# A fused transformer block on one core: one of three small matrix-vector products leaves TensorE for VectorE

## The chip, the cores and the metric

The kernel runs on one core of one Trainium2 chip. The metric is device time in microseconds (us), one number for each execution. Executions of one kernel differ by a few tenths of a microsecond, so I quote medians.

## The reference

A DiT block: two layernorms, each modulated by a shift and a scale that come from a condition vector `c`, attention with two heads, and an MLP. Sizes are B=2, N=256 tokens, D=1152, F=4608.

```python
mod = (_silu(c) @ w_mod).reshape(B, 6, 1, D)
shift_a, scale_a, gate_a, shift_m, scale_m, gate_m = [mod[:, i] for i in range(6)]
h = _layernorm(x) * (1 + scale_a) + shift_a
q, k, v = split(h @ wqkv)                      # H = 2 heads, Dh = 576   (cut)
a = softmax(q k^T * Dh ** -0.5) v @ wo         # (cut)
x = x + gate_a * a
h2 = _layernorm(x) * (1 + scale_m) + shift_m
m = _gelu(h2 @ w_fc1) @ w_fc2
return x + gate_m * m
```

The change is about `mod`: six products of a 2 x 1152 matrix (two batch entries) with a 1152 x 1152 matrix. They need few multiplications, but each needs 2.65 MB of weights to pass through some engine.

## The kernel before

A small scheduler inside the kernel decides, at build time and by a cost model, the order of the instructions on VectorE, ScalarE and GpSimd. The order on TensorE and of the loads is that of the program text. `S.order_after(u, v)` adds a constraint by hand.

Three of the six products, gate_a, shift_m and scale_m, are made together on TensorE in `rows()`. The stationary operand is the two columns of silu(c). The weights stream past it. The 3456 output columns are dealt to four column tiles of the array (`tile_position`, j) and two PSUM banks (r), 448 at a time:

```python
RW = 448
def rows():
    for kt in range(KT):                               # KT = 9 slices of 128 input rows
        for r in range(2):
            for j in range(4):
                c0 = 2 * RW * j + RW * r
                n = min(RW, 3 * D - c0)
                bank = (3, 4)[r]
                mm(psum[32 * j:32 * j + 2, bank * 512:bank * 512 + n], ST[:, kt:18:9], WMODR[:, kt, c0:c0 + n],
                   kt == 0, kt == KT - 1, tile_position=(0, 32 * j))
    ...                                                # evict to ROWS; store gate_a, load it broadcast

def rows_T():                                          # shift_m, scale_m as columns: 18 tiny matmuls
    for i in range(2 * KT):
        j, o = (KT + i) // 7, (KT + i) % 7
        mm(ps32(5, i * 2, 2), ROWS[0:98, o * 128:(o + 1) * 128], IDENT[0:98, 32 * j:32 * j + 2], ...)
    ...                                                # SHM, and SC1M = 1 + scale_m
```

gate_m is already made on VectorE during the MLP, with one multiply-add over a 128 x 1152 slice for each of 9 slices and 2 batch entries:

```python
e.scalar_tensor_tensor(out=acc, in0=w, scalar=s, in1=acc, op0=ALU.mult, op1=ALU.add)   # acc f32, w bf16
```

Then `transpose` and `tensor_reduce` add up within groups of 32 partitions, and one small fp32 matmul adds the groups.

The order on TensorE is: K products; Q products; half products of attention (the 64-row rest of each head); scores and V products, mixed with the transposes of the softmax results; `rows`; the remaining V products and `rows_T`; attention times V; output projection Wo, mixed with the transposes of the second layernorm's tiles; the MLP.

## Time and profile before

| | before |
|---|---|
| time, median of 3 | 246.57 us (246.51 to 246.89) |
| span in the profile, granted clock | 244.6 us, 0.999 |
| busy: TensorE, VectorE, ScalarE | 98%, 40%, 26% |

The first lines of the page of the kernel before are busy time by engine (`PE` is TensorE, `PEld` its weight loads, `DVE` VectorE) and the chain of work that ended last:

```profile
span 244.6 us, 4029 instructions
## 1 busy us (share of the span) xinstructions
PE 239.7 (98%) x1751; PEld 147.4 (60%) x1761; DVE 97.9 (40%) x199; ACT 63.0 (26%) x126; POOL 21.3 (9%) x37
...
PE 95%; DVE 3%; POOL 1%; issue 1%; ACT 0%; DVEq 0%; POOLq 0%
```

TensorE is the bottleneck. Idle time on the other engines is free here, and a saving counts only if it is TensorE time. (In all views, `issue` is time in which an engine waited for nothing that the profile shows.)

The timeline of the kernel before, weight loads only, gives the start of each stage. The columns are start, duration, engine and line, operation, shapes, and in brackets the idle time before and what ended it. `64*128` are the half products, `128*2` the rows, `128*64` the first attention-times-V products; line L690 is a transpose, here the first tile of the second layernorm:

```profile
47.01 0.33 PEld L687 LDWEIGHTS psum<-arena 64*128 64x128 bf16 x8 [0.42 <-issue]
...
66.17 3.12 PEld L687 LDWEIGHTS psum<-arena 128*2 128x2 bf16 x72 [0.32 <-issue]
...
69.67 7.55 PEld L687 LDWEIGHTS psum<-arena 128*128 128x128 bf16 x63 [0.38 <-issue]
...
77.55 0.36 PEld L687 LDWEIGHTS psum<-arena 128*64 128x64 bf16 x8 [0.32 <-issue]
...
94.61 0.65 PEld L690 LDWEIGHTS psum<-arena 128*128 128x128 bf16 x9
```

The rows occupy TensorE from 66.17 to 69.67 us: 3.50 us for 72 matmuls. One after another, they would need about 13 us (an estimate: in this trace 512-wide matmuls start 0.216 us apart). So the tiles run side by side. That is what the Trainium skill, "TensorEngine Tiling (Array Packing)", section Key Properties, says: different tiles can execute weight loads and matmuls in parallel.

The timeline of VectorE shows the room there is. An eviction is the copy of a finished result out of PSUM. Before the Q evictions VectorE idles for 10.57 us:

```profile
45.18 2.63 DVE L684 CAST arena<-psum 128x512 bf16<-128x512 f32 x4 [10.57 <-PE psum L687]
```

The groups of instructions give the prices of the method used for gate_m (`|` busy us, mean ns `|` idle before):

```profile
L1044 DVE SCALAR_TENSOR_TENSOR arena<-arena 128x1152 f32<-128x1152 bf16 x16 | 22.7, 1416 | 0.5
L1048 DVE STREAM_TRANSPOSE arena<-arena 128x1152 f32<-128x1152 f32 x2 | 2.8, 1375 | 0.0
L1050 DVE TENSOR_REDUCE arena<-arena 128x72 f32<-128x2304 f32 x1 | 2.6, 2553 | 0.0
L1041 DVE TENSOR_SCALAR arena<-arena 128x1152 f32<-128x1152 bf16 x2 | 1.6, 812 | 0.0
```

### The profile page before, as it was taken

How to read it: one execution, taken by the hardware profiler on the slowest of the kernel's cores; microseconds unless marked ns; L12 is line 12 of the kernel's file. 1: busy time of each engine (PE TensorE's matmuls, PEld its weight loads, DVE VectorE, ACT ScalarE, POOL GpSimd, SP SyncE). 2: the span in 40 equal slices, each digit the busy share in tenths (PEclk: the TensorE clock that was granted, in tenths of full speed). 3: DMA queues.
4: the chain of work that ended last, by engine and by line, in shares of the span. 5: the costliest groups of instructions: out<-in, count | busy, mean ns of one | idle time of the engine just before them, and what ended most of it. 6: DMA issues, size and time to landing. Idle time of an engine off the chain costs nothing.

```text
span 244.6 us, 4029 instructions
## 1 busy us (share of the span) xinstructions
PE 239.7 (98%) x1751; PEld 147.4 (60%) x1761; DVE 97.9 (40%) x199; ACT 63.0 (26%) x126; POOL 21.3 (9%) x37
## 2 busy tenths in 40 slices
PE   7999999999999999999999999999999999999995
PEld 2698754556656756898544444444556656656575
DVE  3814360455313679879999600000022222111112
ACT  5730340244311306983322333222000000000000
POOL 1500000000021176500000000020000000000000
PEclk9999999999999999999999999999999999999999
DMA  6999999999992999989943589003000000000100
GB/s 242 332 381 392 391 390 406 419 419 405 385 323 66 339 377 392 392 295 398 350 133 97 181 285 343 0 3 96 0 16 19 16 16 20 16 16 16 32 19 19
DMA packets 28844, 51.59 MB, mean 211 GB/s; under 512 B 1559, under 2 KB 15643, under 8 KB 28827
## 3 DMA queue, kind: packets, MB, share of 16 engines
q1 hardware_dynamic: 28384, 50.14, 56.9%
q0 software_dynamic: 416, 1.19, 1.9%
q8 instruction: 14, 0.23, 0.4%
q14 instruction: 3, 0.02, 0.0%
q10 hardware_dynamic: 27, 0.00, 0.0%
HBM read 50.14 MB, written 1.19 MB: 210 GB/s over the span
## 4 chain that ended last, share of the span: by engine, by line
PE 95%; DVE 3%; POOL 1%; issue 1%; ACT 0%; DVEq 0%; POOLq 0%
PE psum L687 93%; PE psum L690 2%; DVE arena L734 1%; DVE arena L755 1%; POOL arena L738 0%; POOL arena L746 0%; DVE arena L735 0%; POOL arena L710 0%; DVE arena L800 0%; DVE arena L737 0%; DVE arena L1233 0%; DVE arena L1234 0%; POOL arena L709 0%; ACT arena L723 0%; DVE arena L724 0%
## 5 line engine op out<-in xcount | busy, mean ns | idle before, releaser
L687 PE MATMUL psum<-arena 128*128 128x384 bf16 (+11 forms) x1662 | 236.0, 309 | 2.0 <-POOL arena L710 1.4
L687 PEld LDWEIGHTS psum<-arena 128*128 128x128 bf16 (+2 forms) x1672 | 142.2, 97 | 91.8 <-issue 4.3
L1233 DVE TENSOR_TENSOR arena<-psum,arena 128x384 f32<-128x384 f32 (+3 forms) x14 | 7.0, 500 | 68.0 <-PE psum L687 68.0
L1143 ACT ACTIVATE arena<-psum 128x512 bf16<-128x512 f32 (+1 forms) x44 | 22.4, 519 | 42.7 <-PE psum L687 42.7
L684 DVE CAST arena<-psum 128x512 bf16<-128x512 f32 (+4 forms) x22 | 13.8, 633 | 31.8 <-PE psum L687 31.7
L682 ACT ACTIVATE arena<-psum 128x512 bf16<-128x512 f32 (+6 forms) x27 | 15.2, 578 | 38.0 <-PE psum L687 35.5
L1044 DVE SCALAR_TENSOR_TENSOR arena<-arena 128x1152 f32<-128x1152 bf16 x16 | 22.7, 1416 | 0.5
L1111 POOL TENSOR_TENSOR arena<-arena 128x384 f32<-128x384 f32 x12 | 10.9, 910 | 12.6 <-DVE arena L1110 10.4
L668 POOL DMA_DIRECT2D dit_scratch<-arena x3 | 1.8, 617 | 116.6 <-ACT arena L682 59.8
L734 DVE BATCH_NORM_STATS2 arena<-arena 128x6 f32<-128x384 f32 (+1 forms) x18 | 9.6, 549 | 0.0
L1056 DVE CAST arena<-psum 72x32 bf16<-72x32 f32 x1 | 0.2, 188 | 21.2 <-PE psum L687 21.2
L1110 DVE TENSOR_TENSOR arena<-psum,arena 128x384 f32<-128x384 f32 x12 | 6.7, 555 | 3.8 <-PE psum L687 3.8
L1116 ACT ACTIVATE arena<-arena 128x1152 bf16<-128x1152 f32 x4 | 5.3, 1344 | 9.8 <-DVE arena L1115 9.8
L690 PE MATMUL psum<-arena 128*128 128x128 bf16 (+1 forms) x89 | 7.3, 219 | 0.2
L690 PEld LDWEIGHTS psum<-arena 128*128 128x128 bf16 (+1 forms) x89 | 5.7, 98 | 2.6 <-DVE arena L755 0.9
L1234 DVE TENSOR_TENSOR arena<-arena 128x384 bf16<-128x384 f32 (+3 forms) x14 | 7.0, 500 | 0.5
L1133 ACT ACTIVATE arena<-psum,arena 128x128 bf16<-128x128 bf16 x16 | 6.1, 454 | 2.8 <-PE psum L690 2.2
L1130 DVE TENSOR_SCALAR arena<-psum,arena 128x128 bf16<-128x128 bf16 x20 | 5.5, 336 | 1.9 <-PE psum L690 1.9
L974 ACT ACTIVATE arena<-psum,arena 128x256 bf16<-128x256 f32 x8 | 3.7, 469 | 7.3 <-DVE arena L971 4.6
L970 DVE TENSOR_REDUCE arena<-psum 128x2 f32<-128x512 f32 x4 | 2.8, 692 | 2.6 <-PE psum L687 2.6
L738 POOL TENSOR_TENSOR arena<-arena 128x1 f32<-128x1 f32 x6 | 3.5, 576 | 1.1 <-DVE arena L737 1.1
L927 ACT ACTIVATE arena<-arena 128x256 bf16<-128x256 bf16 x6 | 2.5, 495 | 4.0 <-DVE arena L921 4.0
(45 smaller groups left out, 42.5 us busy)
## 6 DMA issues: line engine op xcount, KB each, us to landing
arena<-in_w_mod_dram SPq DMA_DIRECT2D x4, 2592.0 KB, 20.9
arena<-in_w_fc_dram SPq DMA_DIRECT2D x9, 1152.0 KB, 8.1
arena<-in_w_fc_dram SPq DMA_DIRECT2D x4, 2592.0 KB, 17.2
arena<-in_wqkv_dram SPq DMA_DIRECT2D x18, 288.0 KB, 11.0
arena<-in_w_mod_dram SPq DMA_DIRECT2D x3, 864.0 KB, 14.0
arena<-in_wqkv_dram SPq DMA_DIRECT2D x1, 2592.0 KB, 12.7
arena<-in_wo_dram SPq DMA_DIRECT2D x1, 2592.0 KB, 32.8
arena<-in_w_mod_dram SPq DMA_DIRECT2D x3, 480.0 KB, 10.2
```

Of the source, the lines that this page charges most:

```text
L682: act(c_act(n), lambda e: e.activation(out=dst, in_=src, func=ACTF.Copy), [src], [dst], name)
L684: dve(c_dve_psum16(n) if psum16 else c_dve_psum32(n), lambda e: e.tensor_copy(dst, src), [src], [dst], name)
L687: S.instr(lambda e: e.matmul(o, lhsT=l, rhs=r, start=st, stop=sp, **kw), reads=[l, r], writes=[o])
L690: S.instr(lambda e: e.transpose(o, i_, idn), reads=[i_, idn], writes=[o])
L734: dve(550, lambda e, s=s, o=o: e.bn_stats(out=o, in_=s), [s], [o], "bn_%s_%d" % (tag, ci))
L1044: dve(1270, lambda e, w=w, s=s, acc=acc: e.scalar_tensor_tensor(out=acc, in0=w, scalar=s, in1=acc, op0=ALU.mult, op1=ALU.add), [w, s, acc] ...
L1110: dve(550, lambda e, o=o, ga=ga, x1c=x1c: e.tensor_tensor(out=x1c, in0=o, in1=ga, op=ALU.mult), [o, ga], [x1c], "wo_t1_%d_%d" % (t, ci))
L1111: S.op("pool", 930, lambda e, xs=xs, x1c=x1c: e.tensor_tensor(out=x1c, in0=x1c, in1=xs, op=ALU.add), reads=[x1c, xs], writes=[x1c], name=" ...
L1133: act(440, lambda e, o=o, dst=dst, s1=s1, s2=s2: e.activation(out=dst, in_=o, func=ACTF.Identity, scale=s1, bias=s2), [o, s1, s2], [dst], ...
L1143: act(c_act(ntok), lambda e: e.activation(out=dst, in_=o, func=ACTF.Gelu_apprx_tanh), [o], [dst], "gelu_%d_%d" % (f, tok0))
L1233: dve(c_dve_psum32(w), lambda e, o=o, gm=gm, t1=t1: e.tensor_tensor(out=t1, in0=o, in1=gm, op=ALU.mult), [o, gm], [t1], "fc2_t1_%d_%d" % ( ...
L1234: dve(c_dve_32(w), lambda e, t1=t1, x1c=x1c, ost=ost: e.tensor_tensor(out=ost, in0=t1, in1=x1c, op=ALU.add), [t1, x1c], [ost], "fc2_out_%d ...
```

## The change

The intent is to take scale_m off TensorE. VectorE makes it with the gate_m method, in the stages where it had room: during Q, attention and V. TensorE's rows are left with gate_a and shift_m, 2304 columns, which split into eight pieces of 288. Order constraints place the multiply-adds between VectorE's other work. Two of VectorE's Q evictions and all of its V evictions go to ScalarE. The scale_m slices are loaded between the slices of WQ.

```diff
-        WMODR = wmat(O_R, 3 * D)
+        WMODR = wmat(O_R, 2 * D)
+        WSM = wmat(O_R + 3 * W1, D)
 ...
+        for o in (0, 640):
+            S.op("pool", 100, lambda e, o=o: e.memset(ROWS[:, o:o + 64], 0.0), ...)   # pads of ROWS
 ...
             dma(WQ[:, kt, :], wqkv_v[:, kt, 0:D], P * D * 2, "ld_wq%d" % kt, run=2304)
+            dma(WSM[:, kt, :], wmod_v[:, kt, 4 * D:5 * D], P * D * 2, "ld_sm%d" % kt, run=2304)
 ...
-        RW = 448
+        RW = 288
 ...
-            S.unit("pe", 2 * KT * 27.0, "rowsT")            # 18 matmuls
+            S.unit("pe", (KT + 1) * 27.0, "rowsT")          # 10 matmuls
 ...
+        def row_sums(W, acc2, t2, out, tag):                # the gate_m method, now for both
+            ...
+        def scale_m_columns():
+            p = ps32(0, 0, 72)
+            mm(p, QR, SMS, True, True)                      # fp32, adds the 4 groups of 32 partitions
+            ...                                             # 4 small VectorE ops write SC1M
 ...
+        for u in S.units:
+            if u.eng == "dve" and u.name.startswith("hx_"):
+                S.order_after(by["sm_0_0"], u)
+        for kt in range(KT):
+            S.order_after(by["sm_1_%d" % kt], by["sm_0_%d" % kt])
+        for j in (0, 2, 4):
+            S.order_after(by["qk_ev%d" % j], by["sm_1_2"])
+            S.order_after(by["sm_0_3"], by["qk_ev%d" % j])
+        S.order_after(by["smax_3"], by["sm_1_4"])
+        S.order_after(by["sm_0_5"], by["spn_3"])
+        ...                                                 # the half sums after the OT evictions
```

More of the change, by code (lines that the diff above doesn't have):

```diff
@@ L598, in build_kernel @@
         WV = wmat(O_C, D)
-        WMODR = wmat(O_R, 3 * D)
+        WMODR = wmat(O_R, 2 * D)
+        WSM = wmat(O_R + 3 * W1, D)
+        SMA = sb(O_R + 2 * W1, 9216, F32)
+        SMT = sb(O_R + 3 * W1 - 9216, 9216, F32)
         WGM = wmat(O_R + 3 * W1, D)
@@ L618, in build_kernel @@
         XN2 = [sb(O_R + 3 * W1 - (i + 1) * 2304, 2304) for i in range(4)]
-        ROWS = sb(O_R + 3 * W1 - 5 * 2304, 1792)
+        ROWS = sb(O_R + 2 * W1 + 9216, 2 * 704)
         GMA = sb(O_X, 9216, F32)
@@ L650, in build_kernel @@
         QS = sb(misc(128), 128, F32)
+        QR = sb(misc(512), 512, F32)
+        SMS = sb(misc(288), 288, F32)
         GMO = sb(misc(64), 64)
@@ L714, in build_kernel @@
         S.op("pool", 100, lambda e: e.memset(NHALF, -0.5), writes=[NHALF], name="nhalf")
+        for o in (0, 640):
+            S.op("pool", 100, lambda e, o=o: e.memset(ROWS[:, o:o + 64], 0.0), writes=[ROWS[:, o:o + 64]], name="rowpad%d" % o)
         dve(270, lambda e: e.memset(Q4B, 0.0), [], [Q4B], "zq4b")
@@ L726, in build_kernel @@
         dve(200, lambda e: e.tensor_reduce(out=QS, in_=i3, axis=AX.X, op=ALU.add), [IDENT], [QS], "qs")
+        q4 = QS.unsqueeze(1).broadcast_to([P, 4, 32])
+        dve(200, lambda e: e.tensor_copy(QR.rearrange("p (a i) -> p a i", a=4), q4), [QS], [QR], "qr")
         dve(170, lambda e: e.scalar_tensor_tensor(out=ST, in0=TH, scalar=1.0, in1=HC, op0=ALU.add, op1=ALU.mult), [TH, HC], [ST], "c_silu")
@@ L892, in qk_evac @@
         def qk_evac(j, bank):
-            copy_on("act" if ev_rr[0] % 2 == 0 else "dve", QK[:, j, :], ps32(bank), 512, False, "qk_ev%d" % j)
+            copy_on("act" if ev_rr[0] % 2 == 0 or j in (6, 8) else "dve", QK[:, j, :], ps32(bank), 512, False, "qk_ev%d" % j)
             ev_rr[0] += 1
@@ L918, in build_kernel @@
         for k0 in range(0, KT, 3):
-            dma(WMODR[:, k0:k0 + 3, :], wmod_v[:, k0:k0 + 3, 2 * D:5 * D], 3 * P * 3 * D * 2, "ld_modr%d" % k0)
+            dma(WMODR[:, k0:k0 + 3, :], wmod_v[:, k0:k0 + 3, 2 * D:4 * D], 3 * P * 2 * D * 2, "ld_modr%d" % k0)
         MT1 = ps32(2, 0, 18)
@@ L998, in v_proj @@
                 mm(o, HX[:, kt, t * 128:(t + 1) * 128], WV[:, kt, ci * CH:(ci + 1) * CH], kt == 0, kt == KT - 1)
-            copy_on("act" if v_rr[0] % 2 else "dve", V[:, t, ci * CH:(ci + 1) * CH], o, CH, False, "v_ev%d_%d" % (t, ci))
-        RW = 448
+            copy_on("act", V[:, t, ci * CH:(ci + 1) * CH], o, CH, False, "v_ev%d_%d" % (t, ci))
+        RW = 288
+        ROWP = 64
         def rows():
@@ L1009, in rows @@
                         c0 = 2 * RW * j + RW * r
-                        n = min(RW, 3 * D - c0)
                         bank = (3, 4)[r]
-                        mm(psum[32 * j:32 * j + 2, bank * 512:bank * 512 + n], ST[:, kt:18:9], WMODR[:, kt, c0:c0 + n],
+                        mm(psum[32 * j:32 * j + 2, bank * 512:bank * 512 + RW], ST[:, kt:18:9], WMODR[:, kt, c0:c0 + RW],
                            kt == 0, kt == KT - 1, tile_position=(0, 32 * j))
             for r, eng in ((0, "act"), (1, "dve")):
-                copy_on(eng, ROWS[0:98, r * RW:(r + 1) * RW], ps32(3 + r, 0, RW)[0:98, :], RW, False, "rows_ev%d" % r)
-            dma(scratch[0, :, 0:2 * RW], ROWS[0:2, :], 2 * 2 * RW * 2, "st_ga0", eng="pool")
-            dma(scratch[0, :, 2 * RW:D], ROWS[32:34, 0:D - 2 * RW], 2 * (D - 2 * RW) * 2, "st_ga1", eng="pool")
+                copy_on(eng, ROWS[0:98, ROWP + r * RW:ROWP + (r + 1) * RW], ps32(3 + r, 0, RW)[0:98, :], RW, False, "rows_ev%d" % r)
+            for j in range(2):
+                dma(scratch[0, :, 2 * RW * j:2 * RW * (j + 1)], ROWS[32 * j:32 * j + 2, ROWP:ROWP + 2 * RW], 2 * 2 * RW * 2, "st_ga%d" % j, eng="pool")
             gate_load(0, GA)
@@ L1024, in rows_T @@
         def rows_T():
-            S.unit("pe", 2 * KT * 27.0, "rowsT")
-            for i in range(2 * KT):
-                j, o = (KT + i) // 7, (KT + i) % 7
-                mm(ps32(5, i * 2, 2), ROWS[0:98, o * 128:(o + 1) * 128], IDENT[0:98, 32 * j:32 * j + 2], i == 0, i == 2 * KT - 1,
-                   skip_group_check=True)
-            a, b_ = ps32(5, 0, 18), ps32(5, 18, 18)
-            dve(170, lambda e: e.tensor_copy(SHM, a), [a], [SHM], "shm")
-            dve(170, lambda e: e.tensor_scalar(out=SC1M, in0=b_, scalar1=1.0, scalar2=None, op0=ALU.add), [b_], [SC1M], "sc1m")
+            S.unit("pe", (KT + 1) * 27.0, "rowsT")
@@ new lines, in rows_T @@
+            for i in range(KT):
+                for j in (2, 3):
+                    c0 = ROWP + 128 * i - 2 * RW * (j - 2)
+                    if -ROWP < c0 < ROWP + 2 * RW:
+                        mm(ps32(5, i * 2, 2), ROWS[0:98, c0:c0 + 128], IDENT[0:98, 32 * j:32 * j + 2], i == 0 and j == 2, i == KT - 1,
+                           skip_group_check=True)
+            a = ps32(5, 0, 18)
+            dve(170, lambda e: e.tensor_copy(SHM, a), [a], [SHM], "shm")
+        def row_sums(W, acc2, t2, out, tag):
+            for kt in range(KT):
+                for b in range(2):
+                    acc = acc2[:, b * D:(b + 1) * D]
+                    w, s = W[:, kt, :], ST32[:, b * KT + kt:b * KT + kt + 1]
+                    if kt == 0:
+                        dve(760, lambda e, w=w, s=s, acc=acc: e.tensor_scalar(out=acc, in0=w, scalar1=s, scalar2=None, op0=ALU.mult),
+                            [w, s], [acc], "%s_%d_%d" % (tag, b, kt))
+                    else:
+                        dve(1270, lambda e, w=w, s=s, acc=acc: e.scalar_tensor_tensor(out=acc, in0=w, scalar=s, in1=acc, op0=ALU.mult, op1=ALU.add),
+                            [w, s, acc], [acc], "%s_%d_%d" % (tag, b, kt))
+            for b in range(2):
+                acc, t = acc2[:, b * D:(b + 1) * D], t2[:, b * D:(b + 1) * D]
+                dve(1270, lambda e, acc=acc, t=t: e.transpose(t, acc), [acc], [t], "%s_tr%d" % (tag, b))
+            for b in range(2):
+                t, o = t2[:, b * D:(b + 1) * D].rearrange("p (c i) -> p c i", i=32), out[:, b * 36:(b + 1) * 36]
+                dve(1270, lambda e, t=t, o=o: e.tensor_reduce(out=o, in_=t, axis=AX.X, op=ALU.add), [t], [o], "%s_sum%d" % (tag, b))
@@ new lines, in scale_m_columns @@
+        def scale_m_columns():
+            S.unit("pe", 300.0, "sm_T")
+            p = ps32(0, 0, 72)
+            mm(p, QR, SMS, True, True)
+            for a in range(4):
+                src = p[32 * a:32 * a + 32, :].rearrange("p (b k a) -> p a k b", b=2, a=4)[:, a]
+                dst = SC1M[32 * a:32 * a + 32, :].rearrange("p (k b) -> p k b", b=2)
+                dve(170, lambda e, src=src, dst=dst: e.tensor_scalar(out=dst, in0=src, scalar1=1.0, scalar2=None, op0=ALU.add), [src], [dst],
+                    "sc1m_%d" % a)
@@ L1034, in gate_m_sums @@
         def gate_m_sums():
             wfc2_load(2)
-            for b in range(2):
-                acc = GMA[:, b * D:(b + 1) * D]
-                for kt in range(KT):
-                    w, s = WGM[:, kt, :], ST32[:, b * KT + kt:b * KT + kt + 1]
-                    if kt == 0:
-                        dve(760, lambda e, w=w, s=s, acc=acc: e.tensor_scalar(out=acc, in0=w, scalar1=s, scalar2=None, op0=ALU.mult),
-                            [w, s], [acc], "gm_%d_%d" % (b, kt))
-                    else:
-                        dve(1270, lambda e, w=w, s=s, acc=acc: e.scalar_tensor_tensor(out=acc, in0=w, scalar=s, in1=acc, op0=ALU.mult, op1=ALU.add),
-                            [w, s, acc], [acc], "gm_%d_%d" % (b, kt))
@@ L1046, in gate_m_sums @@
-            for b in range(2):
-                acc, t = GMA[:, b * D:(b + 1) * D], GMT[:, b * D:(b + 1) * D]
-                dve(1270, lambda e, acc=acc, t=t: e.transpose(t, acc), [acc], [t], "gm_tr%d" % b)
-            t, o = GMT.rearrange("p (c i) -> p c i", i=32), GMS
-            dve(2500, lambda e: e.tensor_reduce(out=o, in_=t, axis=AX.X, op=ALU.add), [t], [o], "gm_sum")
+            row_sums(WGM, GMA, GMT, GMS, "gm")
         def gate_m_rows():
@@ L1152, in build_kernel @@
             qk_evac(j, qb[j])
+        row_sums(WSM, SMA, SMT, SMS, "sm")
         proj(WQ, 6, 6, HX, 0)
@@ L1195, in build_kernel @@
         wo_tile(1)
-        wo_tile(2)
+        wo_tile(2, {1: scale_m_columns})
         xn2_T(0)
@@ L1242, in build_kernel @@
         S.order_after(by["rstd_ln1_2"], by["rstd_ln1_3"])
+        for u in S.units:
+            if u.eng == "dve" and u.name.startswith("hx_"):
+                S.order_after(by["sm_0_0"], u)
+        for kt in range(KT):
+            S.order_after(by["sm_1_%d" % kt], by["sm_0_%d" % kt])
[4 more added lines that the diff above has]
+        S.order_after(by["sm_0_5"], by["spn_3"])
+        for u in S.units:
+            if u.eng == "dve" and u.name.startswith("OT_ev"):
+                S.order_after(by["sm_sum0"], u)
+                S.order_after(by["sm_sum1"], u)
         S.schedule()
```

## The prediction

> **What bounds the kernel now.** TensorE. The page gives it 239.7 of 244.6 us (98%), granted clock 0.999; the chain of waits that ended last is 95% TensorE, after a layernorm head of about 10 us. VectorE is busy 40%, ScalarE 26%. DMA is full (about 400 GB/s) until 67 us, but the chain names none. So only TensorE time counts, unless VectorE or a load becomes late.
>
> **Removed from TensorE.** The row product of gate_a, shift_m, scale_m: 72 matmuls with 2 weight columns each. The timeline puts their weight loads at 66.17 us over 3.12 us. Serial 448-wide matmuls would need about 13 us (a 512-wide one takes 0.215 us), so four column tiles run side by side, as the Trainium skill's "TensorEngine Tiling (Array Packing)", Key Properties, says. The unit costs 18 steps of the widest piece, about 0.187 us: 3.4 us. At 288 columns a step is 0.121 us: 2.2 us. A third less work saves only **1.2 us**. The transposition goes from 18 to 10 tiny matmuls (18 took about 0.55 us): **0.2 us**.
>
> **Added to TensorE.** One fp32 product, 128x72; the similar gate_m one occupies about 0.25 us: about **0.3 us**. A GpSimd memset before the identity may add 0.05 us.
>
> **Added to VectorE.** By the groups of gate_m: 2 scalings at 0.81, 16 multiply-adds at 1.42, 2 transposes at 1.37, 2 half sums at about 1.28: 29.6 us. It loses 6 V evictions (0.56) and 2 Q evictions (0.69) to ScalarE. Busy about 98 to 123 us.
>
> **Does it fit?** The new order on the old timeline:
> - Three pairs (7.3 us) run from 34.6 to about 42, before the Q evictions at 45.2, where VectorE idles 10.6 us.
> - Four multiply-adds fall between softmax steps. Estimates: heads normalised at 54.2, 56.5, 60.0, 61.4; TensorE transposes them at 59.2, 60.9, 62.6, 64.2.
> - Eight more end about 74, transposes 77.0; the first attention eviction is due about 76.7: late by 0.3 us, not seen by TensorE.
> - The half sums delay the first Wo multiplications about 1 us; four PSUM banks absorb it. The first tile of the second layernorm should be ready about 92, needed 93.4.
>
> **DMA.** Bytes are equal, but each WQ slice is followed by a scale_m slice: WQ slices land every 1.5 instead of 0.76 us; Q consumes one each 1.29 us from 33.6. From the cumulative GB/s of the slices and the shift weights' arrival at 29.7, the last should land about 42.3, needed 43.9: slack 1.6 us. V's weights: about 49, needed 53.4; the rows': 62, needed 66.
>
> **Sum.** 246.57 − 1.2 − 0.2 + 0.3 = **245.4 us** (0.5% faster); range **244.8 to 246.5**. Chances: faster by over 2% 0.01, within 2% 0.97, slower 0.02.
>
> **What would show it.** Row weight loads span about 2.0 instead of 3.12 us; TensorE busy falls about 1 us; VectorE's idle time before the Q evictions shrinks from 10.6 to about 3 us; no TensorE wait on VectorE in attention; VectorE near 50%.
>
> **What would make it wrong.** WQ slices late: TensorE waits on a w_qkv load in Q (1 us eats the gain). Softmax late by over 2 us: waits at its transposes. Multiply-adds slower than 1.42 us beside full DMA: attention evictions and second layernorm slip. ScalarE late with all V evictions. Narrow tiles bound by weight loading (28 to 43 ns each): then a row step does not shrink to 0.121 us and little is gained.

## More of the kernel before

The end of the kernel, in the timeline, is VectorE's last addition and the last store's issue (by `SPq`, SyncE's queue). From 242.62 us, the end of that addition, to the end of the span is 1.96 us. I call this the tail.

```profile
242.39 0.23 DVE L1234 TENSOR_TENSOR arena<-arena 128x64 bf16<-128x64 f32 x1
242.71 0.33 SPq L668 DMA_DIRECT2D out_dram<-arena  x1
```

## The result, and the profile after

The changed kernel took 245.87 us (245.64 to 245.98, 4 runs) against 246.55 us (246.51 to 246.89, 4 runs): ratio 0.9968, 95% interval 0.9951 to 0.9985. A second measurement, with other runs of before, gave 245.58 us (245.37 to 245.82, 5 runs) against 246.93 us: ratio 0.9944, interval 0.9932 to 0.9955. A ratio here is the mean time of one kernel's fast runs over that of the other's of the same rounds, so it is not quite the ratio of the medians quoted. By the two measurements the gain is 0.3% and 0.6%; the prediction was 0.5%.

The page after:

```profile
span 243.9 us, 4070 instructions
## 1 busy us (share of the span) xinstructions
PE 239.0 (98%) x1755; PEld 147.4 (60%) x1755; DVE 120.9 (50%) x218; ACT 66.5 (27%) x134; POOL 21.3 (9%) x39
```

The stages in the timeline after, weight loads:

```profile
47.13 0.33 PEld L692 LDWEIGHTS psum<-arena 64*128 64x128 bf16 x8 [0.42 <-issue]
...
66.29 2.06 PEld L692 LDWEIGHTS psum<-arena 128*2 128x2 bf16 x72 [0.32 <-issue]
...
68.60 7.35 PEld L692 LDWEIGHTS psum<-arena 128*128 128x128 bf16 x55 [0.25 <-issue]
...
76.27 0.36 PEld L692 LDWEIGHTS psum<-arena 128*64 128x64 bf16 x8 [0.32 <-issue]
...
93.51 0.65 PEld L695 LDWEIGHTS psum<-arena 128*128 128x128 bf16 x9
```

And the end, in the timeline after:

```profile
241.29 0.23 DVE L1260 TENSOR_TENSOR arena<-arena 128x64 bf16<-128x64 f32 x1
241.63 0.72 SPq L673 DMA_DIRECT2D out_dram<-arena  x1
```

Subtracting start times in the two timelines gives the difference stage by stage:

| stretch | before, us | after, us | difference |
|---|---|---|---|
| start to half products (the head) | 47.01 | 47.13 | +0.12 |
| half products to rows | 19.16 | 19.16 | 0.00 |
| rows | 3.50 | 2.31 | -1.19 |
| rows to attention times V (holds `rows_T`) | 7.88 | 7.67 | -0.21 |
| attention times V to first layernorm tile (holds the fp32 product) | 17.06 | 17.24 | +0.18 |
| first layernorm tile to the end of VectorE's last addition | 148.01 | 148.01 | 0.00 |
| that end to the end of the span (the tail) | 1.96 | 2.39 | +0.43 |
| sum | 244.58 | 243.91 | -0.67 |

The predicted terms are all there (-1.19, -0.21, +0.18 against -1.2, -0.2, +0.3), and nothing else between the half products and the last addition moved. From here on I use that whole stretch as the measure of the core of a kernel: before 242.62 - 47.01 = 195.61 us, after 241.52 - 47.13 = 194.39 us, a difference of -1.22 us. Two terms at the ends were not in the prediction. The tail is 0.43 us longer: its last store took 0.72 us to issue instead of 0.33. The head is 0.12 us longer.

VectorE after: the idle time before the Q evictions is 3.55 us, because six of the new instructions now run there (two multiplications, which start the two sums, and four multiply-adds).

```profile
34.64 0.82 DVE L1051 TENSOR_SCALAR arena<-arena 128x1152 f32<-128x1152 bf16 x1
35.49 1.42 DVE L1054 SCALAR_TENSOR_TENSOR arena<-arena 128x1152 f32<-128x1152 bf16 x1
36.82 0.81 DVE L1051 TENSOR_SCALAR arena<-arena 128x1152 f32<-128x1152 bf16 x1
37.55 4.19 DVE L1054 SCALAR_TENSOR_TENSOR arena<-arena 128x1152 f32<-128x1152 bf16 x3
45.30 1.88 DVE L689 CAST arena<-psum 128x512 bf16<-128x512 f32 x3 [3.55 <-PE psum L692]
```

My theory at this point: the gain is TensorE's alone, it is set by the widest piece of each row step, and VectorE's 24 us of new multiply-adds (and 5.4 us of transposes and sums) cost nothing because every deadline is met. The 0.43 us of tail come from the last store meeting something. The rivals: the sums or the mixed loads take TensorE time back somewhere; the rows' cost goes with the number of matmuls; the tail is chance.

### The profile page after: what moved, and what is told of

Same layout as the page of the kernel before. It is cut to its first block, busy times and chain, and to the rows that moved or that the text cites. A ratio compares the mean times of both kernels' runs of the same rounds, so it can differ in the third digit from the quotient of the medians.

```text
span 243.9 us, 4070 instructions
## 1 busy us (share of the span) xinstructions
PE 239.0 (98%) x1755; PEld 147.4 (60%) x1755; DVE 120.9 (50%) x218; ACT 66.5 (27%) x134; POOL 21.3 (9%) x39
## 3 DMA queue, kind: packets, MB, share of 16 engines
q0 software_dynamic: 416, 1.19, 1.6%
HBM read 50.14 MB, written 1.19 MB: 210 GB/s over the span
## 4 chain that ended last, share of the span: by engine, by line
PE 91%; DMA 5%; SPq 2%; issue 0%; DVE 0%
PE psum L692 90%; DMA arena<-in_w_mod_dram 5%; SPq L673 2%; PE psum L695 1%; DVE arena L1259 0%; DVE arena L1260 0%
## 5 line engine op out<-in xcount | busy, mean ns | idle before, releaser
L692 PE MATMUL psum<-arena 128*128 128x384 bf16 (+12 forms) x1666 | 235.8, 308 | 1.9 <-POOL arena L715 1.5
L692 PEld LDWEIGHTS psum<-arena 128*128 128x128 bf16 (+4 forms) x1666 | 142.2, 97 | 91.3 <-issue 4.7
L1054 DVE SCALAR_TENSOR_TENSOR arena<-arena 128x1152 f32<-128x1152 bf16 x32 | 44.7, 1413 | 0.6
L687 ACT ACTIVATE arena<-psum 128x512 bf16<-128x512 f32 (+6 forms) x35 | 19.0, 560 | 39.8 <-PE psum L692 39.1
L689 DVE CAST arena<-psum 128x512 bf16<-128x512 f32 (+3 forms) x14 | 8.9, 645 | 11.9 <-PE psum L692 11.9
L695 PE MATMUL psum<-arena 128*128 128x128 bf16 (+1 forms) x89 | 7.1, 219 | 0.0
L695 PEld LDWEIGHTS psum<-arena 128*128 128x128 bf16 (+1 forms) x89 | 5.8, 98 | 2.0 <-issue 0.8
L1061 DVE TENSOR_REDUCE arena<-arena 128x36 f32<-128x1152 f32 x4 | 5.4, 1346 | 0.0
L1058 DVE STREAM_TRANSPOSE arena<-arena 128x1152 f32<-128x1152 f32 x4 | 5.4, 1363 | 0.0
```

The lines of the kernel that those rows point to most:

```text
L687: act(c_act(n), lambda e: e.activation(out=dst, in_=src, func=ACTF.Copy), [src], [dst], name)
L689: dve(c_dve_psum16(n) if psum16 else c_dve_psum32(n), lambda e: e.tensor_copy(dst, src), [src], [dst], name)
L692: S.instr(lambda e: e.matmul(o, lhsT=l, rhs=r, start=st, stop=sp, **kw), reads=[l, r], writes=[o])
L695: S.instr(lambda e: e.transpose(o, i_, idn), reads=[i_, idn], writes=[o])
L1054: dve(1270, lambda e, w=w, s=s, acc=acc: e.scalar_tensor_tensor(out=acc, in0=w, scalar=s, in1=acc, op0=ALU.mult, op1=ALU.add), [w, s, acc] ...
```

## The experiments

Twelve runs in four groups. Each group ran on another chip; each run was timed against runs of before on the same chip (median 246.93 to 246.95 us in all four groups), and each has one profile. "Core" and "tail" are the stretches defined above.

| run | median us | ratio to before (95%) | head | core | tail |
|---|---|---|---|---|---|
| before, first profile | 246.57 | | 47.01 | 195.61 | 1.96 |
| changed, first profile | 245.87 | 0.9968 (0.9951-0.9985) | 47.13 | 194.39 | 2.39 |
| e1 narrow alone | 245.71 | 0.9951 (0.9937-0.9964) | 47.07 | 194.21 | 2.20 |
| e2 wide rows | 246.69 | 0.9991 (0.9978-1.0003) | 47.23 | 195.58 | 2.01 |
| e3 two tiles | 245.38 | 0.9937 (0.9925-0.9950) | 47.26 | 194.38 | 2.01 |
| e4 cut warm-ups | 245.19 | 0.9934 (0.9921-0.9946) | 47.33 | 194.38 | 2.01 |
| e5 changed again | 245.58 | 0.9944 (0.9932-0.9955) | 47.27 | 194.38 | 2.21 |
| e6 before, cut warm-ups | 246.87 | 1.0000 (0.9988-1.0012) | 46.86 | 195.61 | 1.96 |
| e7 cut, pads on VectorE | 245.42 | 0.9941 (0.9929-0.9953) | 47.68 | 194.39 | 2.01 |
| e8 four more early | 247.26 | 1.0010 (0.9996-1.0024) | 47.25 | 195.79 | 2.45 |
| e9 scale_m loads first | 250.98 | 1.0167 (1.0131-1.0204) | 52.93 | 194.39 | 2.27 |
| e10 scale_m loads last | 245.53 | 0.9942 (0.9927-0.9957) | 47.27 | 194.39 | 2.07 |
| e11 no constraints | 250.32 | 1.0138 (1.0117-1.0160) | 52.02 | 194.47 | 2.17 |
| e12 cut warm-ups again | 245.40 | 0.9934 (0.9920-0.9948) | 47.26 | 194.38 | 2.02 |

The core repeats to 0.01 us from profile to profile, while times spread by about 0.5 us. Where a timing cannot tell two kernels apart, the core often can.

### e1: TensorE's part alone

```diff
 # on the kernel before; loads unchanged
-        RW = 448
+        RW = 288                       # and rows(), rows_T() as in the changed kernel
+            # SC1M = 1 + shift_m: wrong on purpose, no VectorE sums
```

> The kernel before with TensorE's part of the change alone: rows only for gate_a and shift_m in 288-wide pieces, no scale_m sums on VectorE, all loads as before (scale_m's columns are then computed from shift_m, so the result is wrong on purpose). My theory: all of the gain is TensorE time, 1.19 us in the rows and 0.21 us in the transposition, and the VectorE sums cost TensorE only the 0.18 us fp32 product: this kernel should end its last matmul 1.4 us before the kernel before, about 245.2 us, 0.1 to 0.5 us under the changed kernel. Rival: the sums on VectorE or the mixed loads took back about half a microsecond of TensorE time somewhere that I have not seen; then this one is 1 us or more under the changed kernel (244.8 or lower).

Measured: 245.71 us; the result is wrong, as intended. The core is 194.21 us, 1.40 us under before and 0.18 us under the changed kernel, which is the fp32 product. So the VectorE sums, the moved evictions and the other order of loads cost TensorE nothing in the core. The rival needed 244.8 us or less. The expected time, 245.2 us, was missed: the total was not lower than the changed kernel's second measurement (245.58 us). A difference of 0.2 us is below what the timings resolve, so this reading rests on the core.

### e2: the same kernel with wide rows again

```diff
+                        n = 448 if c0 + 448 <= 2 * D else RW
-                        mm(psum[... bank * 512:bank * 512 + RW], ST[:, kt:18:9], WMODR[:, kt, c0:c0 + RW],
+                        mm(psum[... bank * 512:bank * 512 + n], ST[:, kt:18:9], WMODR[:, kt, c0:c0 + n],
```

> The changed kernel, but the row matmuls stream 448 columns again where the tile has them (the surplus columns are ignored, the result is right); everything else is the changed kernel's. If a row step costs its widest piece, the rows take 3.1 us of weight loads again and the kernel is 1.2 us slower than the changed one: about 247.0 us, a little slower than before. If the gain came from anything else (other loads, fewer evictions on VectorE), it stays under 246.3 us.

Measured: 246.69 us, correct, not distinguishable from before. It is 1.1 us slower than the changed kernel (e5), and its core is 1.20 us longer. One of the eight pieces stays 288 wide, but each row step still holds a 448-wide one. With e1, this fixes the origin of the net gain, the width of the row pieces: the other two terms, 0.21 us saved in the transposition and 0.18 us for the fp32 product, nearly cancel.

### e3: two of the four tiles

```diff
-                    for j in range(4):
+                    for j in range(2):          # gate_a only; shift_m wrong on purpose
```

> The changed kernel with only the two column tiles that make gate_a, 36 row matmuls instead of 72 (shift_m is then wrong on purpose). If the four tiles run side by side, dropping two of them saves nothing: weight loads span about 2.0 us still and the time is the changed kernel's within 0.2 us. Rival, that the unit is bound by the number of weight loads or matmuls: the rows halve, 1.0 us less, about 244.9 us.

Measured: 245.38 us. The row weight loads in the timelines of e2 and then of e3:

```profile
66.39 3.12 PEld L692 LDWEIGHTS psum<-arena 128*2 128x2 bf16 x72 [0.32 <-issue]
```

```profile
66.42 2.05 PEld L692 LDWEIGHTS psum<-arena 128*2 128x2 bf16 x36 [0.32 <-issue]
```

Half the matmuls (36 instead of 72) take the same 2.05 us as in the changed kernel (2.06), and the core is unchanged (194.38). The four tiles do run side by side. A row step costs its widest piece: 448 columns in e2, 288 in e3. Between 36 and 72, the number of matmuls or weight loads does not matter here. The consequence for the change is sobering: it removed a third of the columns and saved 1.2 us, while the 24.2 us of multiply-adds (29.6 us with the transposes and sums) that replace them run on another engine.

### e4: the tail

The kernel starts with warm-up matmuls on the identity, in stretches in which TensorE would otherwise idle; their results are not used. This run cuts each into four.

```diff
-            mm(ps32(5), IDENT, Q4B, True, True)
+            for q in range(4):
+                mm(ps32(5, q * 128, 128), IDENT, Q4B[:, q * 128:(q + 1) * 128], True, True)
 # and the same for the other warm-up matmuls
```

> The changed kernel with each of the 512-wide warm-up matmuls of the idle start cut into four 128-wide ones: the same TensorE time, some 54 matmuls and as many weight loads more in the instruction stream, the result right. In the profile after, the last store's issue took 0.72 us against 0.33 before, while a fetch of TensorE instructions ran (from 240.67 us for 1.28 us); the fetches come every 256 TensorE instructions. If that fetch stretched the tail, about 108 instructions more move it roughly 1.5 to 2 us earlier, the last issue is 0.33 us again, and the time falls by 0.3 to 0.4 us to about 245.5. If the stretched issue is chance, the time does not move (245.7 to 246.0) and the tail varies from profile to profile.

Measured: 245.19 us, ratio 0.9934; core 194.38, tail 2.01 us. The DMA records of a profile hold fetches of instructions: 14 of 16384 bytes in the changed kernel, about 1 us each, on one queue. The Trainium skill, "Runtime: NRT & Kernel Launch", section Instruction fetch mechanics, says that the sequencer fetches instructions in 16 KiB blocks of 256 by its own DMA queue. The trace agrees: between its four fetches from 161.7 to 226.4 us, 257, 256 and 258 TensorE instructions start. In the kernel before, the last such fetch ended at 242.44 us, before the last store was issued. In the changed kernel it ran from 240.67 to 241.96 us, and the issue began inside it. In e4 it came at 236.1 us, 4.5 us earlier; I had expected 1.5 to 2 us. Here are the last issue and the tail against the last fetch, for every profile:

| profile | last fetch ends minus issue begins, us | issue took, us | tail, us |
|---|---|---|---|
| before | -0.27 | 0.33 | 1.96 |
| e2 | -0.10 | 0.33 | 2.01 |
| e10 | -0.03 | 0.35 | 2.07 |
| e3, e4, e6, e7, e12 | -4.3 or less | 0.33 | 1.96 to 2.02 |
| e11 | +0.10 | 0.49 | 2.17 |
| e5 | +0.11 | 0.50 | 2.21 |
| e9 | +0.20 | 0.59 | 2.27 |
| e1 | +0.21 | 0.58 | 2.20 |
| changed, first | +0.33 | 0.72 | 2.39 |
| e8 | +0.39 | 0.33 | 2.45 |

Eight profiles without overlap have tails up to 2.07 us; six with overlap have tails of 2.17 us or more. In five of the six, the issue ends 0.38 to 0.40 us after the fetch does (0.38 us in e10 too, whose fetch ended just before the issue began). In e8 the issue itself was short and the tail long all the same, so how the two collide is not settled. That moving the fetch takes the tail back to 2.0 us is shown, by e4, e7 and e12.

### e5: the changed kernel again

The kernel is unchanged.

> The changed kernel itself once more, beside kernels that differ from it by little. Theory of the fixed 0.4 us: in its profile the last store's issue again overlaps a fetch of TensorE instructions near 240.7 us, takes 0.6 to 0.75 us and ends about 0.38 us after the fetch does, and the time from VectorE's last instruction to the end is 2.2 to 2.4 us against about 2.0 in kernels without the overlap. From the half products of attention to the last weight load it takes 193.46 us, as in the first profile. Ratio to before about 0.997 (245.9 to 246.2 if before is 246.9). If the stretched issue was chance, it is 0.33 us here.

Measured: 245.58 us against 246.93. The core is the same to 0.01 us, and the tail is again longer (2.21 us), at a fetch that overlapped less. The stretched issue took 0.50 us, a little less than the range I gave, and the ratio, 0.9944 instead of 0.997, missed too. (The 193.46 us of the expectation run to the start of the last weight load; they were met, and the core ends 0.92 us later.) In the first measurement the changed kernel won 0.8 us of mean time, here 1.4 us. The core says 1.22 us, less 0.25 to 0.43 us at the tail and 0.12 to 0.26 us at the head: the two profiles are 0.67 and 0.72 us shorter than the one of before. The kernel before was itself 0.4 us slower in this group than in the first measurement. The rest of the difference between the two measurements is not explained.

### e6: the kernel before with cut warm-ups

The edit is that of e4, on the kernel before.

> The kernel before with its warm-up matmuls cut in four, the same edit as in the fourth experiment. Its last store's issue was 0.33 us already, after the fetch had ended, so if moving the fetch away is all that the cut does, there is nothing to gain: within 0.2 us of before, tail about 2.0 us. Rival: the cut shortens something else in any kernel (the start, or all the fetches after it), and before gains 0.4 us or more as the changed kernel did.

Measured: 246.87 us, ratio 1.0000. The cut gives the kernel before nothing, and that kernel had no overlap to lose. So the cut is no general speed-up.

### e7: cut, and the pads on VectorE

```diff
-            S.op("pool", 100, lambda e, o=o: e.memset(ROWS[:, o:o + 64], 0.0), ...)
+            dve(100, lambda e, o=o: e.memset(ROWS[:, o:o + 64], 0.0), ...)
```

> The changed kernel with the warm-ups cut in four and the two memsets of the row pads moved from GpSimd, where they stand before the identity, to VectorE after its modulation work. The identity should be ready at 1.36 us again rather than 1.45; the head after it waits for several things, so 0 to 0.1 us of that arrives. Ratio to before about 0.993, like the fourth experiment, beating both kernels: 245.0 to 245.3 if before is 246.9.

Measured: 245.42 us, ratio 0.9941. The first weight load, which waits for the identity, was at 1.42 us again instead of 1.50, and nothing of that arrived: this profile has the longest head of the undisturbed kernels (47.68 us), with two waits of TensorE for slices of weights from DRAM, 0.41 us until 14.5 us and 0.33 us until 19.3 us. So the pads, worth 0.08 us at most, are not what lengthens the head, and moving them is not worth doing.

### e8: where VectorE's slack ends

```diff
-        S.order_after(by["smax_3"], by["sm_1_4"])
-        S.order_after(by["sm_0_5"], by["spn_3"])
+        S.order_after(by["smax_3"], by["sm_1_6"])
+        S.order_after(by["sm_0_7"], by["spn_3"])
```

> The changed kernel with four more of VectorE's multiply-adds (eight instead of four) ordered in among the softmax steps; the same work in all. By the changed kernel's trace, the normalised head results are done 5.9, 5.4, 2.9 and 3.0 us before TensorE transposes them. Four times 1.41 us is more than the later two have: TensorE should wait about 2 to 2.7 us before the third transposition, on VectorE, and the kernel end 2 to 2.7 us later than the changed one. If the softmax chain has more slack than the trace suggests, the time stays within 0.5 us.

Measured: 247.26 us, slower than the changed kernel by 1.7 us, and its whole gain is gone. The core is 1.40 us longer. The waits of e8 from 60 to 66 us, who waited for whom:

```profile
PEld psum L695 <- DVE arena L988: 1.6, 1, 1.6
PE psum L695 <- DVE arena L988: 1.2, 1, 1.2
```

TensorE waits at a transpose (L695) for a normalised softmax result (L988), where I put it, but for less time than I said (2 to 2.7 us). The changed kernel's results are done at 53.6, 55.7, 59.9 and 61.5 us, and transposed at 59.5, 61.1, 62.8 and 64.5 us, so the third has 2.9 us of room. In e8 it is done at 64.3 us: late by 4.4 us and not by four times 1.41, because the scheduler reordered other steps around the added ones, which my sum had held fixed. 4.4 less 2.9 is 1.5 us, about what the core lost. The free room in the softmax was about 3 us, as the trace said.

### e9: all scale_m slices ahead of WQ

```diff
+        for kt in range(KT):
+            dma(WSM[:, kt, :], ..., "ld_sm%d" % kt)
         for kt in range(KT):
             dma(WQ[:, kt, :], ..., "ld_wq%d" % kt)
-            dma(WSM[:, kt, :], ..., "ld_sm%d" % kt)
```

> The changed kernel with all nine scale_m slices loaded ahead of WQ's instead of between them; everything else the same. By my sum of bytes the interleaved order leaves the WQ slices 1.6 to 3.4 us of slack. With 2.65 MB ahead of them, at about 390 GB/s, the first WQ slice lands some 6 us later than without the scale_m loads, about 37 us, while Q starts at 33.7: TensorE should wait 2.5 to 4 us at the start of Q for a w_qkv load, and the kernel be that much slower than the changed one. If the loads had much more slack than I reckon, the time stays within 0.5 us of it.

Measured: 250.98 us, slower than the changed kernel by 5.4 us. The waits of e9 from 30 to 40 us contain the predicted one, at 3.8 us within the range:

```profile
PE psum L692 <- DMA arena<-in_wqkv_dram: 3.8, 1, 3.8
```

The remaining loss has another cause, which the stretches of time show (columns: us; busy time of TensorE, its weight loads, VectorE, ScalarE, GpSimd; granted clock; DMA share; GB/s):

```profile
33.00:37.50 4.50, 0.74 (x4) 0.12 (x2) 4.46 (x13) 2.40 (x6) 0.00 (x0) 1.00 1.06 391
37.50:39.00 1.50, 1.45 (x4) 0.57 (x5) 1.50 (x2) 0.00 (x0) 0.00 (x0) 0.54 1.04 392
39.00:41.00 2.00, 2.00 (x6) 0.69 (x5) 1.96 (x3) 0.00 (x0) 0.00 (x0) 0.50 1.05 392
41.00:43.00 2.00, 2.00 (x11) 0.92 (x10) 0.88 (x1) 0.00 (x0) 0.00 (x0) 0.99 1.06 394
```

After the idle time TensorE ran at half clock for 3.41 us; the 512-wide matmuls started 0.427 us apart instead of 0.216. That costs another 1.7 us (an estimate: half of 3.41). The Trainium skill, "TensorE: Matmul & The Clock Gate", section "Wait — 56ns, not 53.3ns?", gives 426.7 and 215.7 ns for these two spacings, which agrees. A wait on TensorE can thus cost more than its own length.

### e10: all scale_m slices after WQ

```diff
         for kt in range(KT):
             dma(WQ[:, kt, :], ..., "ld_wq%d" % kt)
+        for kt in range(KT):
+            dma(WSM[:, kt, :], ..., "ld_sm%d" % kt)
```

> The changed kernel with the nine scale_m slices loaded after all of WQ. WQ comes as in the kernel before; the first scale_m slice lands about 36 to 37 us instead of before 34.6, so VectorE's first six multiply-adds start up to 2.5 us later and end about 44 us, still before the Q evictions at 45.3. If mixing the two loads costs TensorE nothing (my theory), the time is the changed kernel's within 0.3 us and the stretch from the half products of attention to the last weight load stays 193.46 us. If the mixed loads are what makes the head of the changed kernel 0.1 to 0.4 us longer than before in the profiles, the half products start at 46.9 to 47.0 us instead of 47.1 to 47.3, and the time falls by 0.3 us.

Measured: 245.53 us; core 194.39, head 47.27 us. VectorE's first multiply-add moved from 34.64 to 36.57 us, and it still finished before the Q evictions. Mixing the two loads cost nothing that the timings or the core resolve, and it is not what makes the head longer.

### e11: no order constraints

All the added `S.order_after` lines are taken out.

> The changed kernel without the explicit order constraints on VectorE's multiply-adds: the compile-time scheduler then puts the first three ahead of the shift weights' eviction, one more ahead of the h writes and eight between the h writes and the Q evictions. VectorE runs in order, and the first scale_m slice lands only about 31 us by my sum of bytes: the shift eviction (30.6 us in the changed kernel) should end about 34 us, Q start 3 to 4 us late, and the Q evictions another 1 to 2 us late behind eight multiply-adds of 1.41 us. The kernel should be 3 to 6 us slower than the changed one. If the constraints only tidy up, it stays within 0.5 us.

Measured: 250.32 us, slower than the changed kernel by 4.7 us. The waits of e11 from 28 to 36 us:

```profile
PEld psum L692 <- DVE arena L689: 3.0, 1, 3.0
PE psum L692 <- DVE arena L689: 2.7, 1, 2.7
DVE arena L1051 <- DMA arena<-in_w_mod_dram: 2.5, 1, 2.5
```

VectorE stood at its first multiply (L1051) for 2.5 us until a scale_m slice had landed. The eviction of the shift row (L689) stood behind it, and TensorE waited for that. Then again came 3.41 us at a clock of 0.50; here is a part of it, with the columns of e9:

```profile
36.00:38.00 2.00, 2.00 (x6) 0.76 (x5) 2.00 (x9) 1.78 (x5) 0.00 (x0) 0.50 1.05 389
```

2.7 to 3.0 us of waiting and 1.7 us of slow clock make up the loss. The constraints, not the cost model, make the change work.

### e12: e4 once more

The kernel is that of e4.

> The fourth kernel once more (the changed kernel with its warm-up matmuls cut in four), to see whether its lead over the changed kernel holds. Its first ratio to before was 0.9934, the changed kernel's second 0.9944 and first 0.9968. In the profile the fetch should again lie near 236 us, the last issue take 0.33 us and the tail be 2.0 us. If the cut is worth the 0.2 us that the tails of the profiles show, the ratio is 0.9930 to 0.9942; at 0.9944 or more no gain from the cut is shown.

Measured: 245.40 us, ratio 0.9934 as in the first run of this kernel; last issue 0.33 us, tail 2.02 us. The cut kernel beats the kernel before by 0.66% in two measurements. Its lead over the changed kernel (0.9968 and 0.9944) has the sign and about the size of the shorter tail, but the intervals overlap, so as a timing that lead is not shown.

## Why the prediction was right or wrong

- **Direction and size: right, with some luck.** Predicted 245.4 us, range 244.8 to 246.5; measured 245.87 and 245.58 us. By the medians the gain is 0.68 and 1.35 us, on either side of the predicted 1.17 us. Two errors of the sum work against each other: the fp32 product was taken 0.12 us too dear, and the ends, which it lacks, cost 0.50 to 0.56 us in the profiles.
- **"Four column tiles run side by side ... a step is 0.121 us": right.** The rows fell by 1.19 us (predicted 1.2). e2 gives it back when the pieces are wide again, and e3 shows that even half the matmuls cost the same.
- **The transposition: right**, 0.21 us (predicted 0.2).
- **The fp32 product "about 0.3 us": too large.** It measured 0.18 us in the profile after, and 0.18 us again as e1 against the changed kernel.
- **VectorE "about 98 to 123": right**, 120.9 us; the idle time before the Q evictions is 3.55 us (predicted about 3). The softmax results came within 0.8 us of my estimates. The first attention eviction, which I had 0.3 us late, was not late: VectorE idled 0.70 us before it. e8 shows that the slack is real but not large.
- **The loads: right.** The last WQ slice landed at 41.98 us (predicted 42.3), V's weights at 49.5 (49), the rows' at 62.4 (62); the first tile of the second layernorm was ready at 92.3 (92).
- **"1 us eats the gain" for a late WQ: confirmed in kind.** With 2.65 MB moved ahead of WQ, TensorE waited 3.8 us for the load. The statement was too mild: 3.8 us of waiting cost 5.4 us.
- **What the sum lacked: the ends.** It summed TensorE's core and took head and tail as fixed. The tail grew by 0.25 and 0.43 us in the changed kernel's two profiles, where the last store overlapped a fetch of TensorE instructions. Together with the longer head, this is the difference between the -1.22 us of the core and the -0.67 and -0.72 us of the spans. The head was 46.9 to 47.1 us in the three profiles of kernels without the scale_m sums, and 47.1 to 47.7 us in the nine undisturbed ones with them. e7 and e10 rule out the pads and the mixed loads. The kept traces show where it arises. The first load of `x` landed at 4.31 to 4.41 us in six profiles (all three without the sums; changed, e7 and e9) and at 4.75 to 5.07 us in the other eight, and the last transposes of the first layernorm's results, at about 13 us, come 0.25 us or more later in those eight. The changed kernel itself has both: 4.38 us in its first profile, 4.78 us in e5. In the first, TensorE waited later, for a load of `w_mod`, as the waits from 14 to 22 us show:

```profile
PE psum L692 <- DMA arena<-in_w_mod_dram: 0.4, 1, 0.4
```

So the head goes with the landing of early loads, which differs between profiles of one kernel. Whether the change also makes late landings more frequent stays open.

## What to carry to other kernels

When small matmuls ran in several column tiles at once, they cost the widest piece, not their sum: before moving one of them to another engine, compute what the narrower step saves, which here was 1.2 us for 30 us of VectorE work. Such filler work is free only while every in-order neighbour meets its deadline. Fix its place by explicit order constraints against measured landings and deadlines, since waits of 2.7 and 3.8 us on TensorE each cost another 1.7 us or so at half clock here. And compare two profiles stage by stage, ends included: a difference of 0.4 us can sit in the last store.

## What the Trainium skill lacked or had wrong

- "Runtime: NRT & Kernel Launch", Instruction fetch mechanics, calls the cost of crossing a 16 KiB boundary "mostly hidden". Inside the kernel the runs agree (e4 moved the fetches, and the core stayed at 194.38 us), but at its end a fetch of 0.9 to 1.3 us that overlapped the last store's issue went with a tail of 2.17 to 2.45 us in six profiles, against 1.96 to 2.07 us in eight without overlap.
- "TensorE: Matmul & The Clock Gate", What's actually happening, gives an idle window of about 3.4 us before the clock falls to half. In e11 a shorter gap, 2.7 us between matmuls, was followed by 3.41 us at clock 0.50; in e9 a gap of 3.8 us did the same; a gap of 1.2 us (e8) did not. The length of the slow period agrees with the page's window (3413 ns).
- No page gives a duration for a `scalar_tensor_tensor` with bf16 weights and an f32 accumulator. On 128x1152 it took 1.41 us beside full DMA (about 400 GB/s) and 1.42 us in the MLP.
